# Clustered attention with a gated feed-forward part: P as the stationary operand of P times V, a column of ones beside V, and a turn by DMA

## The chip, the cores and the metric

The kernel runs on one core of a Trainium2 chip. The core has a matrix engine (TensorE: PE in the profile, with its weight loads listed apart as PEld), a vector engine (DVE), a scalar engine (ACT), a general engine (GpSimd: POOL), a synchronisation engine that issues transfers (SP), and 16 DMA engines. Work lies in SBUF (128 partitions); matmuls write into PSUM. The metric is device time in microseconds (us) of one execution, and the time of a kernel is the median of its runs.

## The reference

Four batches of eight heads, 768 tokens, head size 64. Queries and keys are assigned to the nearest of 16 centroids of their head; a query sees only keys of its own cluster. What follows is a feed-forward part over the heads side by side.

```python
q_assign = np.argmax(np.einsum('bhsd,hcd->bhsc', q_n, c_n), axis=-1)
k_assign = np.argmax(np.einsum('bhsd,hcd->bhsc', k_n, c_n), axis=-1)
mask = q_assign[:, :, :, None] == k_assign[:, :, None, :]
scores = np.where(mask, scale * (q @ k^T), -1e9)
attn = softmax(scores)                     # over keys
x = (attn @ v).transpose(0, 2, 1, 3).reshape(3072, 512)
h = x @ w_in                               # 512 -> 2048
return (h / (1 + exp(-h))) @ w_out         # 2048 -> 512
```

## The kernel before

**Tiles.** A pair p is two heads of one batch (16 pairs, four to a batch). A unit n is one pair and one third of its queries (256 of 768 tokens): 48 units, in the order of the list `units`; batch 0 has an order of its own (`SEQ0`). A chunk c is one batch and one third of its tokens (256 tokens, all 512 columns): 12 chunks, each the sum of four units.

**Steps of a unit.** Q and K come as nat, are split into a high and a low half (hl, lines 96 to 103) and turned into abt (features on partitions; by PE for pairs 0 to 3, by DMA at L113 for the others). The logits against the centroids (psL, L156) lead through a chain on DVE (lt, mx, oht, ohu) to one-hot rows beneath abt, so that a single matmul gives scores and mask. Then three steps of `qk` (L214) give st, keys on partitions and queries along the free axis, and `exp` on ACT (L220) turns each st into a P of 128 keys x (2 key tiles x 2 heads x 256 queries) in half precision.

**P times V** (`pv`, L222 to 253) works on two units at once, m. The stationary operand is a 128x32 piece of V (vt, L231) and P streams past, 256 columns each time, into one of four groups of 32 columns of the array: 48 matmuls for the pair of units. The output pv has features on partitions and tokens along the free axis, as the feed-forward part wants it. The softmax sums zz come from a stationary tile of ones of 128x32: 24 matmuls (L248), or, where m is in FAST (1, 2 and 23), 48 (L240), which give each sum on all the partitions where it is needed. Then:

- plain pairs: DVE copies pv to osb (L257) and takes the reciprocal rz of zz (L261); SP writes four rows of it to DRAM as rzd (L265) and reads them back spread over partitions as rzb (L276); POOL (in some places DVE) multiplies osb by rzb into xt (L289).
- FAST pairs: DVE takes the reciprocal over all partitions (rzb, L281) and multiplies straight from pv (L289).

**Feed-forward.** With all four units of a chunk in xt, `unit_a` (L305) makes ph with w_in as the stationary operand, ACT tanh (L311), DVE the gate gt (L314), `unit_b` (L327) makes po with gt as stationary operand and w_out streaming, DVE halves it into ot (L336) and SP stores it (L340). Chunks 10 and 11 (LATE) have their po in buffers of st.

**The order** is made by a list scheduler at build time (`Piece`, `run`, L401 to 502). Each step is a piece with the engines that may take it, a planned length, the pieces it comes after, the buffers it takes and gives, and a rank; at each planned moment an engine takes the ready piece of lowest rank. On the chip each engine works off its list in that order, and a piece that is not ready holds up what stands behind it on the same engine. PE fills planned gaps ahead of the first ph with `keep_warm` matmuls (warm, L297). The planned lengths set only the order.

Transfers: SP issues q, k, the turns by DMA, the one-hot rows, rzd, rzb and the stores; POOL issues v (L88, converting to half precision), w_in (L680) and w_out (L685). Pools of buffers that matter here: moe (PSUM, 3; shared by pv, zz, ph, the turns on PE and some logits), st (PSUM, 2), P (12), xt (5).

Of the kernel before, what the change touches and what calls it, by code (L numbers as in the profile page):

```python
# [11 lines left out]
f32 = mybir.dt.float32  # L12
f16 = mybir.dt.float16
# [6 lines left out]
def kernel(  # L20
# [47 lines left out]
    vts = [const.tile([128, 2, NJ, D], f16, name=f"vt{n}") for n in range(NV)]  # L68
    ones = const.tile([128, 32], f16, name="ones")
# [7 lines left out]
    sts, Ps, pvs, zzs, osbs, rzs, rzbs, xts, gts, phs, tns, pos, ots = ({} for _ in range(13))  # L77
# [8 lines left out]
    def load_v(p):  # L86
        b, r = divmod(p, HB)
        nc.gpsimd.dma_start(  # L88
            vts[p % NV].rearrange("p h j d -> p h (j d)"), v[b, 2 * r : 2 * r + 2].rearrange("h (p j) d -> p h (j d)", j=NJ)
        )  # L90
# [131 lines left out]
    def pv(m, fast):  # L222
        pvt = pvs[m] = ps.tile([128, 2, UQ], f32, name="pv", tag="moe", bufs=3)
        zz = zzs[m] = ps.tile([128, 2, UQ], f32, name="zz", tag="moe", bufs=3)
        kts = [(s, a) for s in range(3) for a in range(2)]
        quarters = [(h, e) for h in range(2) for e in range(2)]
        for j in range(2):
            p = units[2 * m + j][0]
            for s, a in kts:
                for h, e in quarters:  # L230
                    nc.tensor.matmul(  # L231
                        pvt[D * h + 32 * e : D * h + 32 * e + 32, j, :], vts[p % NV][:, h, 2 * s + a, 32 * e : 32 * e + 32],
                        Ps[2 * m + j, s][:, a, h, :], start=(j == 0 and (s, a) == kts[0]), stop=((s, a) == kts[-1]),
                        skip_group_check=True,
                    )
        if fast:
            for j in range(2):
                for s, a in kts:
                    for h, e in quarters:
                        nc.tensor.matmul(  # L240
                            zz[D * h + 32 * e : D * h + 32 * e + 32, j, :], ones, Ps[2 * m + j, s][:, a, h, :],
                            start=(j == 0 and (s, a) == kts[0]), stop=((s, a) == kts[-1]), skip_group_check=True,
                        )
        else:
            for s, a in kts:
                for h, j in quarters:
                    g = D * h + 32 * j
                    nc.tensor.matmul(  # L248
                        zz[g : g + 32, 0, :], ones, Ps[2 * m + j, s][:, a, h, :], start=((s, a) == kts[0]), stop=((s, a) == kts[-1])
                    )  # L250
        for j in range(2):
            for s in range(3):
                Ps.pop((2 * m + j, s))

    def pv_out(m):
        osb = osbs[m] = mp.tile([128, 2, UQ], f32, name="osb", bufs=4)
        nc.vector.tensor_copy(osb, pvs.pop(m))  # L257

    def z_recip(m):
        rz = rzs[m] = mp.tile([128, UQ], f32, name="rz", bufs=2)  # L260
        nc.vector.reciprocal(rz, zzs.pop(m)[:, 0, :])  # L261

    def z_in(m):
        rzd = dr.tile([4, UQ], f32, name="rzd", bufs=4)
        nc.sync.dma_start(rzd, rzs[m][0:128:32])  # L265
        rzs[m] = rzd

    def rzb_of(m):
        if m not in rzbs:
            rzbs[m] = mp.tile([128, 2, UQ], f32, name="rzb", bufs=3)  # L270
        return rzbs[m]

    def z_bcast(m):
        rzb, rzd = rzb_of(m), rzs.pop(m)
        for h in range(2):
            nc.sync.dma_start(  # L276
                rzb[D * h : D * h + D].rearrange("p j x -> p (j x)"), rzd[2 * h : 2 * h + 2].rearrange("(o j) x -> o (j x)", o=1).to_broadcast([D, 2 * UQ])
            )

    def z_fast(m, j):  # L280
        nc.vector.reciprocal(rzb_of(m)[:, j], zzs[m][:, j])  # L281

    def z_mul(m, j, eng, fast):
        p, u = units[2 * m + j]
        b, r = divmod(p, HB)
        c = b * U + u
        if c not in xts:
            xts[c] = mp.tile([128, NR, UQ], f16, name="xt", bufs=5)
        eng.tensor_tensor(  # L289
            out=xts[c][:, r, :], in0=(pvs if fast else osbs)[m][:, j, :], in1=rzbs[m][:, j, :], op=ALU.mult  # L290
        )
# [7 lines left out]
    def unit_a(c, f):  # L299
        if f == 0:  # L300
            gts[c] = mp.tile([128, NFB, UQ], f16, name="gt", bufs=2)
        ph = phs[c, f] = ps.tile([128, 2, UQ], f32, name="ph", tag="moe", bufs=3)
        for e in range(2):
            for r in range(NR):
                nc.tensor.matmul(  # L305
                    ph[:, e, :], win_s[:, r, ts(2 * f + e, 128)], xts[c][:, r, :], start=(r == 0), stop=(r == NR - 1)
                )
# [79 lines left out]
    def centroid_out(eng):  # L387
        copy = eng.copy if eng is nc.scalar else eng.tensor_copy
        for i, dst in enumerate((wh, wl)):
# [5 lines left out]
            "st": 2, "P": 12, "osb": 4, "rz": 2, "rzd": 4, "rzb": 3, "xt": 5, "gt": 2, "tn": 3, "ot": 2}  # L395
# [113 lines left out]
    LEAD, LEAD_V, LEAD_IN = 28, 22, 36  # L509
    FR0 = (-400, -285, -290, -280)  # L510
    RPV = -3
# [3 lines left out]
    FAST = (1,2,23)  # L515
# [23 lines left out]
    nc.vector.memset(ones, 1.0)  # L539
# [80 lines left out]
    exps, pvl, muls = {}, {}, {}  # L620
# [6 lines left out]
    def value_loads(p):  # L627
        b = p // HB
        casts[p] = [Piece(
            {"POOL": 0.74}, lambda e: load_v(p), ([last_pv[p - NV]] if p >= NV else []) + ([nat_in[HB - 1, 1]] if b == 0 else []), (), rank=-7.3 + p if b == 0 else p,  # L630
            when=from_slot(begins[p] - LEAD_V) if b else None, dma=(0.393, 2.2),
        )]

    for n, (p, u) in enumerate(units):
# [10 lines left out]
        if n % 2 == 0:  # L645
            continue
        m, fast = n // 2, n // 2 in FAST
        two = units[n - 1 : n + 1]
        tiles = [("moe", ("pv", m)), ("moe", ("zz", m))]
        x = Piece(  # L650
            {"PE": 2.82 if fast else 2.18}, lambda e, m=m, fast=fast: pv(m, fast),
            [exps[i] for i in range(3 * n - 3, 3 * n + 3)] + [y for o, _ in two for y in casts[o]], tiles,
            [("P", i) for i in range(3 * n - 3, 3 * n + 3)], rank=-20,
        )
        for o, _ in two:
            last_pv[o] = x
        early = n < 12
        if fast:
            zs = [
                Piece({"DVE": 1.72}, lambda e, m=m, j=j: z_fast(m, j), [x], [("rzb", m)], tiles[1:], rank=-350) for j in range(2)  # L660
            ]
            on, give, rank = {"DVE": 0.35}, tiles[:1] + [("rzb", m)], -300
        else:
            o = Piece({"DVE": 0.69}, lambda e, m=m: pv_out(m), [x], [("osb", m)], tiles[:1], rank=RPV if early else -3)
            x = Piece({"DVE": 1.72}, lambda e, m=m: z_recip(m), [x], [("rz", m)], tiles[1:], rank=RPV if early else -3)
            x = Piece({"SP": 0.5}, lambda e, m=m: z_in(m), [x], [("rzd", m)], [("rz", m)], rank=-4, dma=(0.01, 2.5))
# [77 lines left out]
```

## Time and profile before

| what | value |
|---|---|
| median of 3 runs | 340.08 us (339.46 to 340.91) |
| the profiled execution | 341.08 us, of which the span from first to last instruction is 339.1 |
| granted TensorE clock, mean | 0.995 |
| stores of the output after the last matmul (335.5 to 339.1) | 3.6 us |
| DVE: reciprocals of zz, L261 and L281 | 36.7 and 10.1 us busy |
| POOL: multiplies into xt, L289 | 31.6 us busy |
| DMA: packets | 62080, 43.05 MB |

A row of the profile names engine, line, operation, what it writes and reads, the shape and a count; a group's row has busy time, mean length in ns, and the idle time of the engine ahead of it with what ended that. Rows of the timeline begin with start and length in us. PE lists matmuls with their whole latency, so the rate is read from starts, not from lengths.

### The profile page before, as it was taken

Reading aid. Unit: us, or ns where it says so; the run is one execution under the profiler, and the core shown is the slowest. Engines: PE = TensorE matmul, PEld = TensorE weight load, DVE = VectorE, ACT = ScalarE, POOL = GpSimd, SP = SyncE. Lnnn points to the kernel's source line nnn. Section 1 sums busy time; section 2 is a strip of 40 time slices with the busy share of each in tenths; the row PEclk is TensorE's granted clock in tenths of the full one; section 3 lists DMA queues with packets and bytes.
Section 4 is the critical chain, followed back from the end, with each engine's and each line's share of the span. In section 5 each row is a group of like instructions: output and inputs, shape, how many; then the busy total and the mean of one; then the engine's idle time right before and its main releaser. Section 6 shows DMA issues by size and latency. Waiting matters only on the chain.

```text
span 339.1 us, 9192 instructions
## 1 busy us (share of the span) xinstructions
PE 319.2 (94%) x3956; PEld 232.5 (69%) x3956; DVE 227.0 (67%) x318; ACT 237.0 (70%) x275; POOL 51.9 (15%) x74
## 2 busy tenths in 40 slices
PE   7677987999998999999999999999999999999994
PEld 4455775777765777777777767777677687686651
DVE  5999979789566696457568895547544365266631
ACT  5895776966686868658779678758777786873430
POOL 4730010021103210130120320131011001000000
PEclk9999999999997999999999999999999999999999
DMA  7999999637399911435679671473210110210101
GB/s 236 286 239 254 225 175 216 126 74 194 80 279 258 200 37 57 100 90 90 200 232 244 128 163 46 74 143 65 74 44 34 62 45 21 64 64 2 62 33 62
DMA packets 62080, 43.05 MB, mean 127 GB/s; under 512 B 40580, under 2 KB 55768, under 8 KB 62040
## 3 DMA queue, kind: packets, MB, share of 16 engines
q1 hardware_dynamic: 55000, 35.13, 39.7%
q0 software_dynamic: 7040, 7.34, 13.6%
q8 instruction: 31, 0.51, 0.6%
q14 instruction: 9, 0.07, 0.1%
HBM read 32.80 MB, written 6.38 MB: 116 GB/s over the span
## 4 chain that ended last, share of the span: by engine, by line
PE 78%; DVE 12%; DMA 7%; issue 1%; SPq 1%; POOL 0%; ACT 0%; DVEq 0%; POOLq 0%
PE ph L305 25%; PE po L327 23%; PE st L214 15%; PE pv L231 8%; PE zz L248 4%; DVE hl L103 3%; DMA rzb<-rzd 3%; PE psL L156 2%; DMA rzd<-rz 2%; DMA nat<-in_q_dram 2%; DVE abt L206 1%; DVE ohu L188 1%; DVE rzb L281 1%; DVE lt L163 1%; DVE ot L336 1%
## 5 line engine op out<-in xcount | busy, mean ns | idle before, releaser
L220 ACT ACTIVATE P<-st,bias 128x1024 f16<-128x1024 f32 x144 | 156.5, 1113 | 53.7 <-PE st L214 53.3
L314 DVE SCALAR_TENSOR_TENSOR gt<-tn,ph 128x512 f16<-128x512 f32 x96 | 64.8, 684 | 54.4 <-ACT tn L311 53.7
L305 PE MATMUL ph<-xt,win_s 128*128 128x256 f16 x768 | 97.6, 275 | 2.8 <-POOL xt L289 1.5
L327 PE MATMUL po<-wout_s,gt 128*128 128x512 f16 x384 | 95.7, 379 | 1.1 <-DVE ot L336 1.1
L214 PE MATMUL st<-abt 80*128 80x256 f16 x576 | 84.6, 273 | 5.5 <-ACT P L220 2.2
L305 PEld LDWEIGHTS <-win_s 128*128 128x128 f16 x768 | 75.6, 98 | 20.1 <-issue 3.3
L311 ACT ACTIVATE tn<-ph,zbias 128x512 f32<-128x512 f32 x96 | 65.2, 686 | 30.3 <-PE ph L305 25.8
L214 PEld LDWEIGHTS <-abt 80*128 80x128 f16 x576 | 53.7, 97 | 29.4 <-issue 11.5
L289 POOL TENSOR_TENSOR xt<-osb,rzb 128x256 f16<-128x256 f32 x39 | 31.6, 829 | 238.0 <-DMA rzb<-rzd 219.5
L327 PEld LDWEIGHTS <-gt 128*128 128x128 f16 x384 | 37.3, 97 | 30.8 <-issue 1.8
L261 DVE RECIPROCAL rz<-zz 128x256 f32<-128x256 f32 x21 | 36.7, 1749 | 0.0
L231 PE MATMUL pv<-P,vt 128*32 128x256 f16 x1152 | 35.9, 273 | 0.0
L103 DVE SCALAR_TENSOR_TENSOR hl<-nat,hl 128x768 f16<-128x768 f32 x32 | 31.7, 1021 | 4.4 <-ACT hl L96 4.2
L231 PEld LDWEIGHTS <-vt 128*32 128x32 f16 x1152 | 28.6, 97 | 5.4 <-issue 4.6
L336 DVE TENSOR_SCALAR ot<-po 128x512 f32<-128x512 f32 x24 | 16.5, 686 | 22.6 <-PE po L327 22.5
L257 DVE COPY osb<-pv 128x512 f32<-128x512 f32 x21 | 14.5, 690 | 12.7 <-PE pv L231 12.5
L248 PE MATMUL zz<-P,ones 128*32 128x256 f16 x504 | 17.4, 273 | 0.0
L297 PE MATMUL warm<-idle,ident 128*128 128x256 f16 x74 | 13.3, 309 | 1.4 <-POOL ident masks.py:199 1.4
L248 PEld LDWEIGHTS <-ones 128*32 128x32 f16 x504 | 13.5, 97 | 0.3
L96 ACT ACTIVATE hl<-nat 128x768 f16<-128x768 f32 x14 | 11.7, 840 | 1.8 <-DMA nat<-in_q_dram 1.6
L88 POOL DMA_DIRECT2D vt<-in_v_dram x16 | 12.0, 748 | 5.9 <-PE pv L231 3.3
L281 DVE RECIPROCAL rzb<-zz 128x256 f32<-128x256 f32 x6 | 10.1, 1722 | 1.4 <-PE zz L240 1.4
(56 smaller groups left out, 139.7 us busy)
## 6 DMA issues: line engine op xcount, KB each, us to landing
nat<-in_q_dram SPq DMA_DIRECT2D x16, 384.0 KB
nat<-in_k_dram SPq DMA_DIRECT2D x16, 384.0 KB, 4.8
out_dram<-ot SPq DMA_DIRECT2D x24, 256.0 KB, 2.7
rzb<-rzd SPq DMA_DIRECT2D x42, 128.0 KB, 4.1
vt<-in_v_dram POOLq DMA_DIRECT2D x16, 192.0 KB, 4.9
win_s<-in_moe_w_in_dram POOLq DMA_DIRECT2D x4, 512.0 KB, 14.4
wout_s<-in_moe_w_out_dram POOLq DMA_DIRECT2D x4, 512.0 KB, 23.3
abt<-oh SPq DMA_DIRECT2D x48, 24.0 KB, 1.8
```

The lines of the kernel that those rows point to most:

```text
L103: nc.vector.scalar_tensor_tensor(out=hl[:, :, 1, :], in0=nat, scalar=128.0, in1=hl[:, :, 0, :], op0=ALU.mult, op1=ALU.subtract)
L214: nc.tensor.matmul(st[:, a, h, :], ab[0:K, 1, h, ts(2 * s + a, 128)], ab[0:K, 0, h, ts(u, UQ)], start=True, stop=True)
L220: nc.scalar.activation(out=P, in_=sts.pop((n, s)), func=AF.Exp, bias=bias32, scale=ESC)
L231: nc.tensor.matmul(pvt[D * h + 32 * e : D * h + 32 * e + 32, j, :], vts[p % NV][:, h, 2 * s + a, 32 * e : 32 * e + 32], Ps[2 * m + j, s][: ...
L248: nc.tensor.matmul(zz[g : g + 32, 0, :], ones, Ps[2 * m + j, s][:, a, h, :], start=((s, a) == kts[0]), stop=((s, a) == kts[-1]))
L261: nc.vector.reciprocal(rz, zzs.pop(m)[:, 0, :])
L289: eng.tensor_tensor(out=xts[c][:, r, :], in0=(pvs if fast else osbs)[m][:, j, :], in1=rzbs[m][:, j, :], op=ALU.mult)
L305: nc.tensor.matmul(ph[:, e, :], win_s[:, r, ts(2 * f + e, 128)], xts[c][:, r, :], start=(r == 0), stop=(r == NR - 1))
L311: nc.scalar.activation(out=tn, in_=phs[c, f], func=AF.Tanh, bias=zbias, scale=0.5)
L314: nc.vector.scalar_tensor_tensor(out=gts[c][:, 2 * f : 2 * f + 2, :], in0=tns.pop((c, f)), scalar=1.0, in1=phs.pop((c, f)), op0=ALU.add, o ...
L327: nc.tensor.matmul(pos[c, s], gts[c][:, fc, ts(s, 128)], wout_s[:, fc, :], start=(fc == 0), stop=(fc == NFB - 1))
L336: eng.tensor_scalar(out=ot, in0=pos.pop((c, s)), scalar1=0.5, scalar2=None, op0=ALU.mult)
```

## The change

P becomes the stationary operand. For each unit (not each pair of units) 24 matmuls each load a 128x128 tile of P (128 keys x 128 queries) and stream 65 columns past it: the 64 columns of V of that head and key tile, and a column of ones. The output pv has tokens on partitions, and its column 64 is the softmax sum of that token. So zz, its matmuls, the way through DRAM and the multiplies on POOL are gone. On DVE `normalise` takes the reciprocal of four columns (2 token tiles x 2 heads) and multiplies pv by it into xh (tokens on partitions, half precision). xh must be turned into xt, features on partitions: `x_dma` does this on SP with one DMA transpose for a whole chunk, or, for chunks 0 and 11 (XPE), `x_pe` with two times four transposes on PE and `x_out` with two copies on DVE or ACT. V lies in rows of 72 elements of which 64 are loaded and one is set to ones by POOL at the start; a pair's V is now loaded by two DMAs of 128 x 6 rows of 64 elements. The buffers osb, rz, rzd and rzb go; xh (3) comes; xt has 4 instead of 5. The loads of V start 16 st steps ahead of their use rather than 22 (LEAD_V).

```diff
-    vts = [const.tile([128, 2, NJ, D], f16, name=f"vt{n}") for n in range(NV)]
-    ones = const.tile([128, 32], f16, name="ones")
+    VW = 72
+    vts = [const.tile([128, 2, NJ, VW], f16, name=f"vt{n}") for n in range(NV)]
...
-        nc.gpsimd.dma_start(
-            vts[p % NV].rearrange("p h j d -> p h (j d)"), v[b, 2 * r : 2 * r + 2].rearrange("h (p j) d -> p h (j d)", j=NJ)
-        )
+        for h in range(2):
+            nc.gpsimd.dma_start(vts[p % NV][:, h, :, 0:D], v[b, 2 * r + h].rearrange("(p j) d -> p j d", j=NJ))
...
-    def pv(m, fast):
...
+    def pv(n):
+        p, u = units[n]
+        out = pvs[n] = ps.tile([128, 2, 2, D + 1], f32, name="pv", tag="moe", bufs=3)
+        for s in range(3):
+            P = Ps.pop((n, s))
+            for a in range(2):
+                for h in range(2):
+                    for e in range(2):
                         nc.tensor.matmul(
+                            out[:, e, h, :], P[:, a, h, ts(e, 128)], vts[p % NV][:, h, 2 * s + a, 0 : D + 1],
+                            start=(s + a + h + e == 0), stop=(s == 2 and a == 1), skip_group_check=True,
                         )
+    def normalise(n):
...
+        nc.vector.reciprocal(rz, out[:, :, :, D])
+        nc.vector.tensor_tensor(
+            out=xhs[c][:, :, r], in0=out[:, :, :, 0:D], in1=rz.unsqueeze(3).to_broadcast([128, 2, 2, D]), op=ALU.mult
+        )
+    def x_dma(c):
+        nc.sync.dma_start_transpose(xt_of(c).rearrange("p e r x -> p (e r) x"), xhs.pop(c).rearrange("p e r h d -> p (e r h d)"))
+    def x_pe(c, e):
+        xp = xps[c, e] = ps.tile([128, NR, 128], f16, name="xp", tag="moe", bufs=3)
+        for r in range(NR):
+            nc.tensor.transpose(xp[:, r, :], xhs[c][:, e, r].rearrange("p h d -> p (h d)"), ident)
+    def x_out(c, e, eng):
+        copy = eng.copy if eng is nc.scalar else eng.tensor_copy
+        copy(xt_of(c)[:, e], xps.pop((c, e)))
...
-    LEAD, LEAD_V, LEAD_IN = 28, 22, 36
+    LEAD, LEAD_V, LEAD_IN = 28, 16, 36
...
-    FAST = (1,2,23)
+    XPE = (0, 11)
...
+    for vt in vts:
+        nc.gpsimd.memset(vt[:, :, :, D : D + 1], 1.0)
```

With the pieces the scheduler's order changes. The next two pieces are from DVE's list before, and after, from the copies of the one-hot rows of batch 0's last pair (abt from ohu) towards the first xt; hl, from nat, is the split of batch 1's Q and K.

```order
L206 TENSOR_SCALAR abt_380<-ohu_615 16x768 x4
L257 COPY osb_641<-pv_504 128x512
L261 RECIPROCAL rz_652<-zz_505 128x256
L98 TENSOR_SCALAR hl_667<-nat0_473 128x12x64
L98 TENSOR_SCALAR hl_680<-nat1_477 128x12x64
L98 TENSOR_SCALAR hl_781<-nat0_499 128x12x64
L98 TENSOR_SCALAR hl_786<-nat1_502 128x12x64
L98 TENSOR_SCALAR hl_789<-nat0_580 128x12x64
L103 SCALAR_TENSOR_TENSOR hl_667<-nat0_473,hl_667 128x12x64
L281 RECIPROCAL rzb_800<-zz_684 128x256 x2
L289 TENSOR_TENSOR xt_835<-pv_683,rzb_800 128x256 x2
L289 TENSOR_TENSOR xt_848<-osb_641,rzb_792 128x256
```

```order
L205 TENSOR_SCALAR abt_385<-ohu_614 16x768 x4
L97 TENSOR_SCALAR hl_639<-nat0_541 128x12x64
L97 TENSOR_SCALAR hl_666<-nat1_562 128x12x64
L242 RECIPROCAL rz_675<-pv_641 128x4
L243 TENSOR_TENSOR xh_487<-pv_641,rz_675 128x2x128
L102 SCALAR_TENSOR_TENSOR hl_639<-nat0_541,hl_639 128x12x64
L102 SCALAR_TENSOR_TENSOR hl_666<-nat1_562,hl_666 128x12x64
L97 TENSOR_SCALAR hl_727<-nat0_569 128x12x64
L97 TENSOR_SCALAR hl_729<-nat1_572 128x12x64
L242 RECIPROCAL rz_740<-pv_702 128x4
L243 TENSOR_TENSOR xh_487<-pv_702,rz_740 128x2x128
```

The reciprocals of 256 columns and the multiplies into xt are replaced by short pairs of a reciprocal of 4 columns and a multiply into xh, one pair of instructions for each unit, spread between the splits. Two more such pairs (units 0 and 1) stand earlier, inside the routing of the last two pairs of heads. On PE the first ph stands behind 20 groups of st (of four matmuls each) in place of 25.

On SP's list, from the last loads of batch 1 on, before and after:

```order
L83 DMA nat_580<-in_q_dram 128x2x384
L83 DMA nat_582<-in_k_dram 128x2x384
L265 DMA rzd<-rz 4x256
L276 DMA rzb<-rzd 64x512 x2
L83 DMA nat_807<-in_q_dram 128x2x384
L113 DMA_TRANSPOSE abt<-hl 128x12x128
L83 DMA nat_959<-in_k_dram 128x2x384
L113 DMA_TRANSPOSE abt<-hl 128x12x128 x5
```

```order
L83 DMA nat_579<-in_q_dram 128x2x384
L83 DMA nat_586<-in_k_dram 128x2x384
L83 DMA nat_690<-in_q_dram 128x2x384
L112 DMA_TRANSPOSE abt<-hl 128x12x128
L83 DMA nat_738<-in_k_dram 128x2x384
L112 DMA_TRANSPOSE abt<-hl 128x12x128 x6
L253 DMA_TRANSPOSE xt<-xh 128x8x128
L112 DMA_TRANSPOSE abt<-hl 128x12x128
```

The way of the sums through DRAM is gone from SP, and the turn of chunk 1 stands among the turns of batch 1's Q and K. POOL's list before and after, from the end of the centroids' split:

```order
L88 DMA vt_75<-in_v_dram 128x2x384
L88 DMA vt_76<-in_v_dram 128x2x384
L88 DMA vt_77<-in_v_dram 128x2x384
L88 DMA vt_78<-in_v_dram 128x2x384
L680 DMA win_s<-in_moe_w_in_dram 128x2048 x4
L685 DMA wout_s<-in_moe_w_out_dram 128x4x512 x2
L88 DMA vt_79<-in_v_dram 128x2x384
L685 DMA wout_s<-in_moe_w_out_dram 128x4x512 x2
L88 DMA vt_80<-in_v_dram 128x2x384
```

```order
L89 DMA vt_75<-in_v_dram 128x6x64 x2
L89 DMA vt_76<-in_v_dram 128x6x64 x2
L89 DMA vt_77<-in_v_dram 128x6x64 x2
L89 DMA vt_78<-in_v_dram 128x6x64 x2
L642 DMA win_s<-in_moe_w_in_dram 128x2048 x4
L647 DMA wout_s<-in_moe_w_out_dram 128x4x512 x4
L89 DMA vt_79<-in_v_dram 128x6x64 x2
L89 DMA vt_80<-in_v_dram 128x6x64 x2
```

Eight issues for V stand where four stood, all of w_in and w_out behind them, and the V of batch 1's first two pairs behind all of w_out.

127 lines of the change are left out of this document (33 added, 94 removed).

## The prediction

> **What bounds the kernel now.** I read the page first (busy shares, slices, the chain that ended last), then busy time by stretches, then the timeline of TensorE.
>
> ```profile
> span 339.1 us, 9192 instructions
> PE 319.2 (94%) x3956; PEld 232.5 (69%) x3956; DVE 227.0 (67%) x318; ACT 237.0 (70%) x275; POOL 51.9 (15%) x74
> PE ph L305 25%; PE po L327 23%; PE st L214 15%; PE pv L231 8%; PE zz L248 4%; DVE hl L103 3%; DMA rzb<-rzd 3%; PE psL L156 2%; DMA rzd<-rz 2%; DMA nat<-in_q_dram 2%; DVE abt L206 1%; DVE ohu L188 1%; DVE rzb L281 1%; DVE lt L163 1%; DVE ot L336 1%
> ...
> 0.00:54.30 54.30, 42.01 (x600) 31.36 (x601) 47.12 (x85) 41.84 (x50) 13.99 (x26) 1.00 1.06 235
> 250.00:304.80 54.80, 54.80 (x668) 41.34 (x657) 28.21 (x35) 41.13 (x49) 5.22 (x7) 1.00 0.14 49
> 304.80:335.50 30.70, 29.44 (x263) 18.44 (x260) 15.04 (x22) 9.12 (x13) 0.73 (x1) 1.00 0.09 35
> ```
>
> The last three rows are stretches: the bounds, then length, busy us of PE, PEld, DVE, ACT, POOL, then granted clock, DMA share and GB/s. There are two stages. Up to 54.3 us PE is no limit (42.0 of 54.3, warm-up matmuls included), while DVE is busy for 47.1. From 54.3, where the first matmul of the feed-forward part (ph) starts, to the last matmul at 335.5, PE hardly rests: the end is the start of that stage plus the PE work that is then left plus the holes. So the change is to be priced by what it does to PE work after the first ph, to the time of the first ph, and to the holes.
>
> **PE work of P times V.** Timeline rows: start, length, engine, line, what, count.
>
> ```profile
> 155.42 1.04 PE L305 MATMUL ph<-xt,win_s 128*128 128x256 f16 x8
> ...
> 156.73 1.03 PE L327 MATMUL po<-wout_s,gt 128*128 128x512 f16 x4
> 157.59 1.04 PE L305 MATMUL ph<-xt,win_s 128*128 128x256 f16 x8
> ...
> 160.64 0.60 PE L214 MATMUL st<-abt 80*128 80x256 f16 x4
> 161.18 1.49 PE L231 MATMUL pv<-P,vt 128*32 128x256 f16 x48
> 162.50 0.83 PE L248 MATMUL zz<-P,ones 128*32 128x256 f16 x24
> 163.25 0.61 PE L214 MATMUL st<-abt 80*128 80x256 f16 x4
> ...
> 306.74 1.50 PE L231 MATMUL pv<-P,vt 128*32 128x256 f16 x48
> ...
> 309.47 1.04 PE L327 MATMUL po<-wout_s,gt 128*128 128x512 f16 x4
> ...
> 15.27 0.49 PE L118 MATMUL ptt<-ident,hl 128*128 128x128 f16 x6 [0.80 <-ACT abt L123]
> ...
> L118 PE MATMUL ptt<-ident,hl 128*128 128x128 f16 x96 | 6.9, 219 | 3.3 <-ACT abt L123 1.9 <-DVE abt L123 0.9 <-DVE hl L103 0.4
> ```
>
> The lengths hold the pipeline's latency, so starts count. A pair of units costs PE 163.25 - 161.18 = 2.07 us, and another 0.1 where the array changes from full width to 32-column tiles (the four st before it are worth 0.44 and end by that at 161.08): **2.17 per pair**, and 309.47 - 306.74 + 0.1 = **2.83** for a pair with 48 matmuls of zz instead of 24 (three pairs, FAST). Twenty plain pairs and one of those stand behind the first ph: 20 x 2.17 + 2.83 = **46.2 us**.
>
> After, a unit is 24 matmuls, each with its own load of a 128x128 tile of P, and streams only 65 columns. No row shows 65 columns. From the rows: six matmuls of 128 columns take 0.49 us, of which the last one alone is 0.22, so they start (0.49 - 0.22) / 5 = 54 ns apart, 55 with the rounding; eight ph and the four st behind them, all of 256 columns, take 156.73 - 155.42 = 1.31 us, 109 ns each; four po of 512 take 157.59 - 156.73 = 0.86, 215 ns each. That is about 0.42 ns per column and 2 ns more, which gives 65 columns **29 ns**, if the load of P keeps up. For the load:
>
> ```profile
> 309.47 0.11 PEld L327 LDWEIGHTS <-gt 128*128 128x128 f16 x2 [0.21 <-issue]
> ...
> L305 PEld LDWEIGHTS <-win_s 128*128 128x128 f16 x768 | 75.6, 98 | 20.1 <-issue 3.3
> L231 PEld LDWEIGHTS <-vt 128*32 128x32 f16 x1152 | 28.6, 97 | 5.4 <-issue 4.6
> ```
>
> Two loads of 128x128 that wait for nothing between them fit into 0.11 us though each lasts 97, so the second starts about 15 ns behind the first; and a load of 128 columns lasts no longer than one of 32 (98 against 97 ns). The bounds are therefore 29 ns from below and 55 ns, the closest that a load and a matmul of full width are seen to follow each other, from above. I take 29, because the upper row is set by its own 128 columns and the 15 ns of the load fit under 29. Then 42 units x 24 x 29 ns = **29.2 us**, without the change of array shape: 17.0 saved behind the first ph. The turn of chunk 11 on PE (8 transposes of 55 ns) gives back **0.4**.
>
> Here the Trainium skill speaks against the change. "TensorE: Matmul & The Clock Gate", section "Back-to-back issue gap", says that in a stream of load and matmul pairs 128 columns sustain about 81 ns each, 25 above the lone matmul, because the load takes its share. By that a 65-column pair would be some 54 ns (an estimate), and the saving would be gone. The 55 ns that this trace shows at 128 columns speak against the rule.
>
> **When the first ph starts.** Rows of PE, ACT and DVE.
>
> ```profile
> 39.20 1.49 PE L231 MATMUL pv<-P,vt 128*32 128x256 f16 x48
> 40.52 1.48 PE L240 MATMUL zz<-P,ones 128*32 128x256 f16 x48
> 46.76 0.60 PE L214 MATMUL st<-abt 80*128 80x256 f16 x4 [0.19 <-ACT P L220]
> 54.34 0.49 PE L305 MATMUL ph<-xt,win_s 128*128 128x256 f16 x3
> ...
> 32.28 8.35 ACT L220 ACTIVATE P<-st,bias 128x1024 f16<-128x1024 f32 x8 [0.80 <-PE st L214]
> 42.58 6.13 ACT L220 ACTIVATE P<-st,bias 128x1024 f16<-128x1024 f32 x6 [1.95 <-PE st L214]
> ...
> 36.62 0.69 DVE L257 COPY osb<-pv 128x512 f32<-128x512 f32 x1
> 37.23 1.75 DVE L261 RECIPROCAL rz<-zz 128x256 f32<-128x256 f32 x1
> 42.23 3.36 DVE L281 RECIPROCAL rzb<-zz 128x256 f32<-128x256 f32 x2
> ...
> L353 DVE RECIPROCAL cr<-cy 128x1 f32<-128x1 f32 x2 | 0.3, 163 | 0.4 <-ACT cy L363 0.4
> L289 DVE TENSOR_TENSOR xt<-pv,rzb 128x256 f16<-128x256 f32 x6 | 2.1, 384 | 0.0
> ```
>
> Before, the first ph stands behind 25 groups of st; after, behind 20. The 20th starts now at 46.8, paced by ACT at 1.04 us (8.35 / 8), with a gap of 1.95 on ACT that the 2.7 us block of pv and zz at 39.2 causes. Blocks of 24 x 29 ns = 0.7 us hide under one step of ACT, so that gap goes. Against it, two normalisations now stand ahead of the routing of the last two pairs. One is a reciprocal of 4 columns (163 ns at one column; (1749 - 163) / 255 = 6 ns for each further one: 0.18) and a multiply (0.38), so 0.57, and together with the reordering about 0.8 us. The 20th st comes at 46.8 - 1.95 + 0.8 = 45.7; behind it stand its own 0.44, one pv of 0.7, and the wait for normalisation, turn and copy of chunk 0, which I put at 1.2 (a normalisation and a copy of PSUM at 0.6 each): the first ph at **48.0**, 6.3 earlier. The reciprocals of zz on DVE (one more such pair stands between 52.4 and 55.8) are gone from that way. But five groups of st (5 x 0.44 = 2.2) move behind it: **4.1** gained. What is late next is win_s:
>
> ```profile
> q0 software_dynamic: 710, 0.52, 68.3%
> ...
> q1 hardware_dynamic: 144, 0.03, 9.8%
> ...
> L680 POOL DMA_DIRECT2D win_s<-in_moe_w_in_dram x4: 538/567/651, 10.9 to 12.6; - x4
> DMA to landing us min/median/max: 10.7/14.4/18.1
> ```
>
> Its last piece lands at about 12.6 + 18.1 = 30.7, behind four loads of V. A load of V turns from 256 packets (128 partitions x 2 heads) into 1536 (x 6 tiles) of 256 bytes at the source. The rows q0 and q1 are packets and their share of 16 engines in two windows. The 144 of q1 (0.7 to 2.2 us) are craw, rows of 256 bytes from HBM and a few ends: 9.8% of 16 x 1.5 us, so 16 ns each. The 710 of q0 (10 to 15 us), V's of today and some of win_s, take 68.3% of 16 x 5 us, 77 ns each. Four loads cost 4 x 256 x 77 / 16 = 4.9 us of all DMA engines now; after, between 4 x 1536 x 16 / 16 = 6.1 and, at 77, 29.6. I take the craw row, the one of that size: win_s at some 32, covered by the 16 us up to 48. POOL's issues double too (8 for 4); it loses its multiplies for that and has nothing else to do. Its six memsets of the ones column stand ahead of ident, at a time when it waits for the norm of the centroids anyway.
>
> **Holes.** The stage of 281.1 us holds 46.2 of pv and zz, 96 x 0.87 of ph, 96 x 0.87 of po, 119 x 0.44 of st and six logits blocks of 1.41, 274 in all; 7 are holes. Their largest:
>
> ```profile
> 56.12 0.71 PE L305 MATMUL ph<-xt,win_s 128*128 128x256 f16 x5 [1.29 <-DVE xt L289]
> 103.75 2.43 PE L305 MATMUL ph<-xt,win_s 128*128 128x256 f16 x13 [1.19 <-POOL xt L289]
> 147.95 1.41 PE psL L156 x32
> ...
> rzb<-rzd SPq DMA_DIRECT2D x42, 128.0 KB, 4.1
> abt<-hl SPq DMA_TRANSPOSE x24, 4.4
> ```
>
> The waits for xt behind the sums' way are worth 1.3 + 1.2, and 13 matmuls in 2.43 us instead of 12 x 0.11 + 0.27 = 1.6 another 0.8: 3.3 in all. Their path (reciprocal 1.75, a DMA out, 4.1 for the DMA back, a multiply on POOL) becomes 0.57 on DVE and one DMA turn, for which abt gives 4.4. It is shorter, but stands in SP's queue ahead of turns of K and Q, loads and stores, which then wait for the last unit of a chunk. I count half: **1.7**.
>
> **Sum.** The profiled execution took 341.08 (span 339.1 and 2.0 around it). 341.1 - 17.0 + 0.4 - 4.1 - 1.7 = 318.7. The median of the runs (340.08) is 1.0 below that execution: **318** rounded, 6.5% faster. DVE (one reciprocal of 1.75 and a copy of 0.69 less for each pair, two times 0.57 more) and POOL gain besides, but nothing waits for them there, so I cost that at nothing.
>
> **Rivals.** *A, the load is not hidden:* the pair takes 55 ns like the full-width row. Then P times V costs 42 x 24 x 55 = 55.4, 9.2 more than now, and the time is 340.1 + 9.2 + 0.4 - 4.1 - 1.7 = **344**, slower. It decides from (46.2 - 0.4 + 4.1 + 1.7) / 1008 = 51 ns. For it: no row shows the two closer. Against it: the 15 ns between loads, and equal lengths at 32 and 128 columns. *B, V's short packets:* at 77 ns win_s lands at 30.7 + 24.7 = 55.4, the first ph waits 7.4 longer: **325**. For it: DMA is saturated up to 54 us (share 1.06). Against it: craw. *C, ACT becomes the limit in places:* from 250 to 304.8 ACT is busy 41.1 of 54.8 and would have the same work in about 51. A wait of 0.19, as ACT's P causes at 46.76, for each of 42 units is 8 us: **326**. That the change doesn't do what it says I rule out: its matmuls stand in the order as 24 to a unit.
>
> **How the numbers follow.** Forecast (312 to 324) 0.64; B 0.11; C 0.13; A 0.08; and 0.04 for a mixture that lands within 0.5%, about what a measurement of this kernel can tell from no change. The range runs from 312 (all holes gone, the first ph two more us earlier) to 331 (B or C, with 5 more for pairs of 34 ns); A stays outside. Faster 0.88, same 0.04, slower 0.08.
>
> **What would show it.** Starts of pv matmuls 29 ns apart and blocks of 0.7; the first ph near 48; win_s landed before 40; PE full from there on. Over 50 ns, or a first ph past 55 that waits for win_s or vt, and I am wrong.

## The result and the profile after

The changed kernel takes **322.0 us** (median of 4 runs, 319.5 to 323.8) against 339.8 for the kernel before in the same session: 0.9475 of the time, 95% interval 0.9395 to 0.9554. In the next session, as the control of the experiments, it took 321.2 (0.9436, 0.9396 to 0.9476). The forecast was 318, in a range of 312 to 331.

First the page of the changed kernel (span, busy shares, the chain that ended last, two groups), then what the trace answers on the tile win_s.

```profile
span 322.0 us, 7812 instructions
...
PE 302.5 (94%) x3316; PEld 225.5 (70%) x3316; DVE 190.2 (59%) x356; ACT 239.3 (74%) x279; POOL 35.3 (11%) x57
...
PE ph L276 25%; PE po L298 24%; PE st L213 16%; PE pv L229 9%; DMA abt<-hl 6%; PE psL L155 3%; DMA nat<-in_q_dram 2%; DMA xt<-xh 2%; DVE hl L102 1%; DVE abt L205 1%; DVE ohu L187 1%; DVE lt L162 1%; DVE hl L97 1%; DVE mx L173 1%; DVE oht L180 1%
...
L229 PE MATMUL pv<-vt,P 128*128 128x65 f16 x1152 | 43.3, 193 | 0.2 <-ACT P L219 0.2
L229 PEld LDWEIGHTS <-P 128*128 128x128 f16 x1152 | 41.8, 98 | 2.1 <-ACT P L219 0.3
```

```profile
L642 POOL DMA_DIRECT2D win_s<-in_moe_w_in_dram x4: 528/534/552, 15.1 to 18.0; - x4
...
DMA to landing us min/median/max: 10.1/13.2/16.3
```

In the chain zz, rzd and rzb are gone, and a new entry has come: the turn of hl into abt by DMA, with 6%, which did not stand in the chain before. win_s has landed by 18.0 + 16.3 = 34.3, well ahead of the first ph.

The stretches (bounds, length, busy us of PE, PEld, DVE, ACT, POOL, granted clock, DMA share, GB/s):

```profile
0.00:47.68 47.68, 37.64 (x460) 28.24 (x461) 40.17 (x84) 38.88 (x48) 19.04 (x37) 0.96 1.24 236
47.68:53.30 5.62, 2.35 (x26) 1.86 (x22) 1.12 (x4) 3.84 (x5) 0.00 (x0) 1.00 1.61 170
53.30:57.00 3.70, 3.69 (x26) 2.77 (x27) 2.01 (x3) 1.10 (x2) 0.00 (x0) 0.54 1.35 107
...
60.00:155.00 95.00, 95.00 (x1101) 71.92 (x1099) 63.52 (x113) 74.91 (x88) 11.43 (x14) 1.00 0.81 138
155.00:166.00 11.00, 10.14 (x112) 7.58 (x111) 3.10 (x7) 7.97 (x10) 1.63 (x2) 1.00 1.08 234
...
225.00:280.00 55.00, 55.00 (x593) 41.52 (x592) 22.74 (x47) 42.48 (x48) 0.00 (x0) 1.00 0.16 43
```

From 60 to 300 us PE is full but for one wait (0.86 us at 163.4). The trouble lies between 47.7 and 57: PE is busy for 2.35 of 5.62 us, and then, full, runs at a clock of 0.54. The timeline of PE, a piece there and two further on:

```profile
46.95 0.89 PE L229 MATMUL pv<-vt,P 128*128 128x65 f16 x24
47.68 1.04 PE L276 MATMUL ph<-xt,win_s 128*128 128x256 f16 x8
48.55 0.60 PE L213 MATMUL st<-abt 80*128 80x256 f16 x4
48.99 1.04 PE L276 MATMUL ph<-xt,win_s 128*128 128x256 f16 x8
53.31 1.64 PE L276 MATMUL ph<-xt,win_s 128*128 128x256 f16 x8 [3.28 <-DVE xh L243]
...
150.17 0.90 PE L229 MATMUL pv<-vt,P 128*128 128x65 f16 x24
150.90 1.02 PE L298 MATMUL po<-wout_s,gt 128*128 128x512 f16 x4
...
164.25 1.05 PE L276 MATMUL ph<-xt,win_s 128*128 128x256 f16 x8 [0.86 <-DMA xt<-xh]
```

and that of DVE at the same place:

```profile
52.14 0.56 DVE L97 TENSOR_SCALAR hl<-nat 128x768 f16<-128x768 f32 x1 [5.25 <-DMA abt<-hl]
52.62 0.17 DVE L242 RECIPROCAL rz<-pv 128x4 f32<-128x4 f32 x1
52.83 0.42 DVE L243 TENSOR_TENSOR xh<-pv,rz 128x256 f16<-128x256 f32 x1
```

A unit of P times V takes 150.90 - 150.17 = 0.73 us from start to start, 30.4 ns per matmul. PE's wait of 3.28 us at 50.0 is named after xh: the next ph needs a buffer of moe, and the normalisation that writes xh is what gives back the one that pv held. But xh itself was late by the instruction ahead of it: a split of batch 1's Q or K (hl) that stood for 5.25 us until a buffer of hl came free, which a turn by DMA was still reading. The normalisation, 0.59 us of work, stood behind it in DVE's list.

**The account.** Before and after, from the two profiled executions:

| term | forecast | measured |
|---|---|---|
| first ph (54.34 before) | 48.0: -6.3 | 47.68: -6.7 |
| five groups of st behind it (119, then 124) | +2.2 | +2.2 |
| 42 units of P times V (46.2 before) | 29.2: -17.0 | 42 x 0.73 = 30.7: -15.5 |
| turn of chunk 11 on PE | +0.4 | +0.4 |
| holes from the first ph to the last matmul | 7 to 5.3: -1.7 | 7 to 9.2: **+2.2** |
| the end and what lies around the span | 0 | +0.1 |
| sum | -22.4 | -17.3 |

The last matmul ends at 318.0, so that stage has 318.0 - 47.7 = 270.3 us; its work is 30.7 + 192 x 0.87 + 124 x 0.44 + 6 x 1.41 + 0.4 = 261.1, which leaves 9.2. Of these, 3.28 and 0.86 are the two waits shown and 1.1 two waits near the end that the kernel before has too; the stretch at 0.54 costs 1.7 (3.70 x 0.46); the other 2.3 are not traced to a cause. The execution took 323.8, 17.3 less than 341.1.

### The profile page after: what moved, and what is told of

Its sections match the earlier page's. It is cut to its first block, busy times and chain, and to the rows that moved or that the text cites. A ratio compares the mean times of both kernels' runs of the same rounds, so it can differ in the third digit from the quotient of the medians.

```text
span 322.0 us, 7812 instructions
## 1 busy us (share of the span) xinstructions
PE 302.5 (94%) x3316; PEld 225.5 (70%) x3316; DVE 190.2 (59%) x356; ACT 239.3 (74%) x279; POOL 35.3 (11%) x57
## 4 chain that ended last, share of the span: by engine, by line
PE 78%; DMA 9%; DVE 9%; ACT 1%; issue 1%; SPq 1%; DVEq 0%
PE ph L276 25%; PE po L298 24%; PE st L213 16%; PE pv L229 9%; DMA abt<-hl 6%; PE psL L155 3%; DMA nat<-in_q_dram 2%; DMA xt<-xh 2%; DVE hl L102 1%; DVE abt L205 1%; DVE ohu L187 1%; DVE lt L162 1%; DVE hl L97 1%; DVE mx L173 1%; DVE oht L180 1%
## 5 line engine op out<-in xcount | busy, mean ns | idle before, releaser
L89 POOL DMA_DIRECT2D vt<-in_v_dram x32 | 26.5, 833 | 174.0 <-PE pv L229 165.2
L229 PE MATMUL pv<-vt,P 128*128 128x65 f16 x1152 | 43.3, 193 | 0.2 <-ACT P L219 0.2
L229 PEld LDWEIGHTS <-P 128*128 128x128 f16 x1152 | 41.8, 98 | 2.1 <-ACT P L219 0.3
L102 DVE SCALAR_TENSOR_TENSOR hl<-nat,hl 128x768 f16<-128x768 f32 x32 | 29.8, 956 | 2.8 <-ACT hl L95 2.5
L242 DVE RECIPROCAL rz<-pv 128x4 f32<-128x4 f32 x48 | 8.6, 178 | 28.0 <-PE pv L229 27.6
L243 DVE TENSOR_TENSOR xh<-pv,rz 128x256 f16<-128x256 f32 x48 | 20.4, 424 | 1.7
L97 DVE TENSOR_SCALAR hl<-nat 128x768 f16<-128x768 f32 x19 | 10.4, 556 | 5.3 <-DMA abt<-hl 5.2
L155 PE MATMUL psL<-abt,wh 128*32 128x512 f16 (+1 forms) x128 | 10.5, 340 | 0.7 <-DVE abt L122 0.4
L187 DVE STREAM_TRANSPOSE ohu<-oht 128x768 f16<-128x768 f16 x10 | 9.8, 977 | 0.9 <-DVE oht L180 0.5
L117 PE MATMUL ptt<-ident,hl 128*128 128x128 f16 x96 | 7.7, 235 | 2.7 <-ACT abt L122 1.9
```

Of the source, the lines that this page charges most:

```text
L89: nc.gpsimd.dma_start(vts[p % NV][:, h, :, 0:D], v[b, 2 * r + h].rearrange("(p j) d -> p j d", j=NJ))
L102: nc.vector.scalar_tensor_tensor(out=hl[:, :, 1, :], in0=nat, scalar=128.0, in1=hl[:, :, 0, :], op0=ALU.mult, op1=ALU.subtract)
L155: nc.tensor.matmul(psL[g : g + 32, 0 : hi - lo], w, x[:, lo:hi], start=first, stop=last)
L229: nc.tensor.matmul(out[:, e, h, :], P[:, a, h, ts(e, 128)], vts[p % NV][:, h, 2 * s + a, 0 : D + 1], start=(s + a + h + e == 0), stop=(s = ...
L243: nc.vector.tensor_tensor(out=xhs[c][:, :, r], in0=out[:, :, :, 0:D], in1=rz.unsqueeze(3).to_broadcast([128, 2, 2, D]), op=ALU.mult)
```

## Experiments

All but one (7) start from the changed kernel. Times are medians, and the ratios in brackets are to runs of the kernel before in the same session (340.6, 339.6 and 340.4 us in the three sessions; experiments 1, 2, 4 and 5 are from the first). Two questions are open: what sets the 30 ns of a 65-column matmul, and what made the holes. On the first, theory M says that the columns do, its rivals that the load does, or that PE had slack to hide the difference. On the second, theory R says that the ring of hl buffers joins the late turns to PE, theory P that V's short packets make the turns late, and theory H, which came up with the first four runs, that PE's standstills halve its clock in the early stage; the rivals are that the hole only moves, and that it is nothing to the time.

**1. Control.** The changed kernel as it is.

> The changed kernel once more, as the control beside the others on this chip. By its earlier runs about 322 us (319.5 to 323.8), with the hole of about 3.3 us on PE after the second block of ph (near 50 us), where DVE waits some 5 us for a turn of K or Q (abt from hl).

321.2 us (320.6 to 322.2). Its profile differs from the first one: the first ph is at 50.72 instead of 47.68, and there is no hole behind it (264.1 us from there to the last matmul, holes 3.0 instead of 9.2; span 318.8). One program, two courses: an early ph that runs into a hole, and a late one that doesn't. The wait of DVE for a turn is there too, shorter, but PE has work in that time:

```profile
51.65 0.56 DVE L97 TENSOR_SCALAR hl<-nat 128x768 f16<-128x768 f32 x1 [1.92 <-DMA abt<-hl]
```

So a profile without a hole near 50 doesn't by itself show that a repair worked. What delayed the ph is seen in experiment 6.

**2. 128 columns.** `vts[...][:, h, 2*s+a, 0 : D+1]` becomes 128 columns from the same place of a flattened tile, pv becomes 128 wide.

> Each matmul of P times V streams 128 columns instead of 65 (the rest is the neighbouring rows of the V tile, and is not used); the order of PE is unchanged. Theory M (columns set the spacing, the load of P is hidden, PE work passes to the end one for one): matmuls 55 to 56 ns apart for 29, so 42 x 24 x 26 ns = 26 us more, about 348. Rival L (a load and a matmul share the time, the page's 81 ns at 128 columns): 42 x 24 x 52 ns, about 374. Rival O (PE has slack, the added work is partly hidden): below 340.

346.2 us (1.0159, 1.0098 to 1.022). The timeline's piece:

```profile
159.16 1.50 PE L230 MATMUL pv<-vt,P 128*128 128x128 f16 x24
160.50 1.03 PE L299 MATMUL po<-wout_s,gt 128*128 128x512 f16 x4
```

160.50 - 159.16 = 1.34 us, 56 ns per matmul. 42 x (1.34 - 0.73) = 25.6 us more. The time went up by 25.0, and in the profiles the stage from the first ph to the last matmul by 25.7 (289.8 for the control's 264.1): what P times V costs behind the first ph passes to the end one for one, and there is no slack on PE.

**3. 33 columns.** Half of V's columns are left out, so this kernel is for its timing only.

```diff
-  vts[p % NV][:, h, 2 * s + a, 0 : D + 1],
+  vts[p % NV][:, h, 2 * s + a, 32 : D + 1],
```

> The changed kernel with 33 columns instead of 65 streaming past each P tile: half of the value columns (0 to 31) is left out and the other half is used twice, so the normalisation is two products of 128 columns instead of one of 256. Theory M (the columns alone set the spacing, 65 in 30.4 ns and 128 in 56): 33 columns in 15 to 17 ns, 0.36 to 0.41 us per unit, 13 to 15 us less PE work after the first ph, of which ACT (74% busy) lets through most: 307 to 312. Rival L (the load of a 128x128 tile sets a floor of nearly 29 ns, which 65 columns happened to touch): spacing 27 to 29 ns, time 319 to 322.

317.6 us in one run, with the hole near 50 (2.83) as in the profile after.

```profile
164.13 0.76 PE L229 MATMUL pv<-vt,P 128*128 128x33 f16 x24
164.74 1.02 PE L299 MATMUL po<-wout_s,gt 128*128 128x512 f16 x4
```

0.61 us per unit, 25 ns per matmul: neither expectation, and nearer to rival L's. With half of the columns gone only 5 ns went. So 128, 65 and 33 columns take 56, 30 and 25 ns: by columns at first, then hardly. That 25 is a floor, of which 65 columns stay just clear, is how I read it; there is no run below 33 columns.

**4. A sixth buffer of hl** (`name="hl", bufs=5` to 6, the order of all work unchanged).

> One more buffer for hl (6 for 5), the order of every engine unchanged. Theory R (the ring of five hl buffers is where a late turn stops DVE, and with it the normalisation that ph waits for through the PSUM buffers): the DVE wait of 5.2 us and the PE hole of 3.3 us near 50 us go, and with the hole the half clock after it: 3.3 plus some 1.8 of slower matmuls, so about 317. Rival S (DVE would wait for the late transfers at the next instruction anyway, or the PE hole has another cause): the hole stays or moves by a microsecond, 321 to 322.

320.7 us (0.9411, 0.9378 to 0.9445). The first ph is at 48.2, nearly as early as in the first profile, and there is no hole near 50 (no idle of PE over 0.3 us from 45 to 58); DVE's wait for a buffer comes at a later split and is shorter:

```profile
57.50 0.56 DVE L97 TENSOR_SCALAR hl<-nat 128x768 f16<-128x768 f32 x1 [1.61 <-DMA abt<-hl]
```

The turns themselves are as late as ever (12.6 us at worst, 12.2 in the first profile), so it is the buffer that joins them to PE. The median moved by 0.5 us only, within the intervals; the 317 that was expected did not come.

**5. V loads of pairs 4 and 5 held** until the last turn of pair 5 is down (a copy of one column on POOL ahead of them that reads it).

```diff
+        if p == HB:
+            nc.gpsimd.tensor_copy(mp.tile([32, 1], f16, name="after_turn"), abt_of(HB + 1)[0:32, 1, 2 * NJ - 1, 0:1])
```

> The V loads of batch 1's first two pairs (four DMAs of short rows) wait, by a small copy on POOL that reads it, for the last turn of batch 1's second pair; nothing else is moved. Theory P (the short V packets, landing at 40 to 53 us, are what makes the turns of 41 to 52 us late): the first turn lands in some 5 us instead of over 10, the hole near 50 us goes, about 317 to 318. Rival Q (the turns are late because they are issued 4 us earlier than in the kernel before and meet w_out and the q and k loads): the first turns stay late, the hole stays, 321 to 323.

320.1 us (0.9397, 0.9356 to 0.9438). The turns land in 6.8 us at worst instead of 12.2 (9.7 in the control), no split of DVE waits for one any more, and there is no hole near 50; the first ph stands at 49.9. The 1.1 us against the control are within the intervals, and the 317 to 318 of theory P did not come. The two queues between 46 and 52 us (packets, MB, share of 16 engines), after the change and in the combination (9, below) that also holds these loads:

```profile
q1 hardware_dynamic: 1662, 0.57, 93.8%
q0 software_dynamic: 1738, 0.24, 70.5%
```

```profile
q1 hardware_dynamic: 3363, 1.17, 126.9%
q0 software_dynamic: 13, 0.01, 1.1%
```

After the change 1738 short packets of V, only 0.24 MB, take 70.5% of 16 x 6 us, 39 ns each, while SP's queue with the turns (q1) moves 0.57 MB, half of what it moves without them. (The two shares add up to 164%: the times of packets overlap, so 100% is not a ceiling.) In the kernel before, q0 has 10 packets in these 6 us.

**6. Idle matmuls where PE stands still** (12 each ahead of the third block of ptt, the first st, and the first st of pair 2).

```diff
+        if (n, s) in ((0, 0), (2, 0)):
+            keep_warm(12)
...
```

> The changed kernel with 12 idle matmuls (1.3 us at full clock) put ahead of each of the three PE instructions that waited longest in the first 34 us of its profile (the third block of six ptt, the first st, the first st of pair 2), all three behind waits that are there anyway. Theory H (the half clock comes some 2 to 4 us after PE has stood still for over 1.3 us in one piece; without such pieces it isn't halved before the first ph; each halved stretch of 3.4 us makes the PE work that lies in it twice as long and the first ph later): granted clock 1.00 in all of 10 to 48, first ph 47.0 to 48.0, time 319 to 320.5, and a narrower spread over its runs than the control's 320.6 to 322.2. Rival N (PE's stillness has nothing to do with it; the clock is halved by the power of the DMAs or of the chip): half windows as in the control, time 321.0 to 322.0. Rival C (the filled waits were shorter than 1.3 us and the idle matmuls delay the first exp): first ph after 49, time 322 to 323.

322.7 us (0.949, 0.9459 to 0.9521): no gain; by the ratios 1.8 us worse than the control, within the intervals. But the clock did what theory H says. Stretches of PE alone (bounds, length, busy us, granted clock, DMA share, GB/s), the control first:

```profile
8.00:12.00 4.00, 2.10 (x20) 0.69 1.25 350
12.00:16.00 4.00, 4.00 (x42) 0.50 1.99 213
...
32.00:36.00 4.00, 2.04 (x15) 1.00 1.16 264
36.00:40.00 4.00, 3.74 (x27) 0.61 1.24 210
40.00:44.00 4.00, 4.00 (x37) 0.54 1.36 199
```

```profile
8.00:12.00 4.00, 3.65 (x47) 1.00 1.21 353
12.00:16.00 4.00, 3.30 (x49) 1.00 2.00 211
...
32.00:36.00 4.00, 3.01 (x23) 1.00 1.15 255
36.00:40.00 4.00, 3.71 (x50) 1.00 1.24 208
40.00:44.00 4.00, 3.79 (x69) 1.00 1.24 220
...
48.00:52.00 4.00, 1.50 (x15) 1.00 1.47 197
52.00:56.00 4.00, 4.00 (x44) 0.64 1.65 146
```

In the control two stretches in which PE works for 2.0 or 2.1 of 4 us run into some 7 us at half clock each; with the idle matmuls neither comes, and the first ph is at 46.7, 4.0 earlier than in the control (and 1.0 earlier than in the first profile, which has one such stretch, from 12.6 to 16.0). All of it is then lost: the earlier ph runs into the late turn (a hole of 2.5 at 49.1), and the half clock comes after that.

**7. V's short rows alone, in the kernel before** (rows of 72, two DMAs a pair).

> The kernel before with one part of the change alone: V is loaded into rows of 72, in two DMAs per pair with descriptors of 256 B instead of one with 3 KB (32 DMAs instead of 16, the products unchanged). Theory P (the short rows cost nothing by themselves in the middle of the program; they only hold up what shares the DMA engines in the first 15 us and around the last loads and turns before the first ph): first ph 54 to 56, time 340 to 343, ratio 1.00 to 1.008. Rival (the loads themselves are a cost of 7 us, rival B of the prediction): first ph after 58, time 347. Rival (no effect at all, the late turns of the changed kernel have another cause): turns of hl land within 5 us as in the kernel before, and the time is 340.0 to 340.5.

345.7 us, 1.018 (1.0136 to 1.0224): **6.1 us slower**. The size is that of the rival, the place that of theory P: the first ph is at 54.1, as before the change, and the loss comes behind it.

```profile
57.80 1.23 PE L304 MATMUL ph<-xt,win_s 128*128 128x256 f16 x5 [3.22 <-DVE xt L288]
```

This wait was 1.29 in the kernel before; half clock from 56 to 63 begins in it. On DVE the multiplies that it waits for are late because an earlier one, ahead of them on the list, waits 3.83 us for the sums' way through DRAM (rzb), against 1.88 before. In the two profiles the stage from the first ph on is 4.3 us longer (285.3 for 281.0), which the wait and the half clock cover; the medians differ by more. So a new form of V's loads that the sum had at nothing costs 6 us in the old surroundings.

**8. V loaded in one piece and spread by POOL** (a staging tile, then `nc.gpsimd.tensor_copy` into the rows of 72).

> The changed kernel with V loaded as before the change (one DMA per pair, 3 KB per partition in one piece) into a staging tile, and copied from there by POOL into the rows of 72 (about 1 us of POOL per pair, in which POOL issues no DMA); the planner puts a few blocks after the first ph in another order. Theory P (the short rows cost 6.1 us in the kernel before, through one late product ahead of the second ph block and a half-clock stretch behind it; in the changed kernel they cost the late turns of hl near 50 us in the same way): turns land within 6 us, no hole over 1 us between 45 and 60, time 317 to 319. Rival (holding back the V loads of pairs 4 and 5 alone has already taken what there was, 1.1 us of 321.2): 319.5 to 320.5. Rival (POOL's copies come late and hold up pv): a pv behind POOL in the waits, time over 321.

323.6 us (0.9518, 0.9472 to 0.9564), and the turns land in 10.6 at worst, with a hole of 2.83 at 52.2. That speaks against theory P as I had put it: the rows are long again, and the turns as late. Between 46 and 52 us:

```profile
q0 software_dynamic: 880, 0.65, 69.0%
q1 hardware_dynamic: 1281, 0.65, 55.7%
```

The software queue is as full there as with the short rows, now with 0.65 MB, because POOL's copies stand ahead of its issues: win_s is issued from 20.4 on instead of 15.1, and what follows moves with it. What the profiles with late turns have in common is therefore not the row but the **backlog of the software queue when batch 1's turns begin**; short rows are one way to it, late issues another. That is argued, not shown: experiment 5 shows that the turns come sooner when V's loads are held, but no run separates the form of the loads from their place. After the change the V of batch 1's first two pairs is issued from 25.4 to 35.4, behind all of w_out; before, at 17.5 and 24.9.

**9. The parts together.** Sixth buffer, held V loads, idle matmuls:

> The combination without the later rank of the first 12 normalisations: the sixth hl buffer, the V loads of pairs 4 and 5 held, and the idle matmuls (12, 12, 12); the order of all other work is that of the changed kernel. If the earlier exp chain (normalisations off batch 0's routing) carries the combination's 317.4: first ph near 47, time 319 to 320. If the turns in time and the full clock carry it (theories R, P and H): first ph at 46.5 to 47.5, no hole, no half clock, time 317.5 to 318.5. Alone, the idle matmuls gave a first ph at 46.7 and then a hole of 2.5 at 49.1 with half clock behind it, 322.7.

**317.6 us** (0.9332, 0.9298 to 0.9365). First ph at 46.0, no hole over 0.7 us but the one ahead of the last po that the kernel before has too, clock 1.00 in every stretch, the turns within 9.1, and no split of DVE waits for one:

```profile
0.00:46.00 46.00, 40.36 (x496) 30.85 (x497) 40.43 (x85) 38.69 (x48) 15.69 (x33) 1.00 1.20 241
46.00:60.00 14.00, 14.00 (x179) 11.49 (x179) 9.00 (x18) 13.83 (x17) 3.57 (x6) 1.00 1.32 196
```

The same, with the first 12 normalisations ranked behind batch 0's routing on DVE (`rank=-300` to -270) and 6 idle matmuls instead of 12 ahead of pair 2:

> Everything that the runs so far point to, together: the sixth hl buffer, the V loads of pairs 4 and 5 held until the turns of pair 5 are down, the idle matmuls of the run before (6 instead of 12 ahead of pair 2), and the first 12 normalisations ranked behind batch 0's routing on DVE, so that nothing stands between the rows abt L205 of a pair. Theory H with R and P: first ph at 46 to 47.5, no hole over 0.5 us after it but the tail's, granted clock 1.00 from 10 on, time 315.5 to 318. Rival (the first ph is bounded by ACT's exp chain, whose start is all that the normalisations moved, and a hole that goes comes back at the next late turn): 319 to 320.5, as each part alone.

317.4 us (0.9346, 0.9321 to 0.9372), first ph at 45.4: no difference that these runs can tell. The last one with the staged loads of 8 in place of the held ones:

> The combination with the staged V loads in place of the held ones: sixth hl buffer, idle matmuls, later normalisations, V loaded in one piece per pair and spread by POOL. Theory P: the same turns in time, and no held loads: first ph at 45 to 46.5, time 315.5 to 317.5. Rival (POOL's copies delay its other issues, win_s and w_out among them): win_s lands after 36 and the time is 318 to 320.

320.9 us (0.941, 0.9364 to 0.9456), 0.9 above the range of its rival, with win_s down by 36.2, as that said. In its profile the clock is half from 20.7 to 27.5, with the idle matmuls in place. So the combination without the rank is the version that beats both kernels, by 3.6 us against the control (by the ratios, 0.9436 and 0.9332, 3.5), clear of the intervals: more than its three parts alone (0.5, 1.1 and -1.5, none clear of noise) add up to. The profiles fit this: an earlier first ph was lost where a split then waited for a turn (experiment 6) and kept where none did (here). No run leaves one of the three parts out, so which of them the 3.6 needs is not shown.

**10. All chunks turned by PE** (`XPE = tuple(range(12))`), the DMA turn of the change undone.

> The changed kernel with all 12 chunks turned by PE (8 transposes of 128x128 each and two copies by DVE or ACT) instead of two by PE and ten by DMA. By the prediction's price for a turn on PE (0.4 us per chunk beside the copies) ten more cost 4 to 4.5 us, against which stand the waits for a turned chunk (0.86 at 164) and the DMA time that the turns take from those of hl: theory S (PE's work passes to the end): 324 to 326. Rival T (the late turns of hl come from the turns of x on the same queue): hole at 50 gone and time 320 to 322.

324.5 us in 2 runs (0.953, 0.9471 to 0.9589), 3.3 above the control, as theory S; the hole near 51 is still there (1.28) and the turns of hl land in 12.3 at worst, so the turns of x aren't what makes those of hl late.

## Why the prediction held, and where it did not

**P times V: right in mechanism, 1.5 us too low.** The saving is what the change is worth, and it passes to the end one for one (experiment 2). The sum had 29 ns; the starts are 29 apart in the median, but with some at 35 the mean is 30.4. That 29 was made of 0.42 ns per column and 2 more, with the load hidden; the run at 33 columns shows that such a line does not go on below (16 ns by it, 25 measured). The forecast lay 5 ns above those 25, of which its rows knew nothing: that the line still held at 65 was luck.

**Rival A, the load not hidden, is rejected**: 30 ns at 65 columns with a load of 128x128 each, and 56 only at 128 columns. The Trainium skill, "TensorE: Matmul & The Clock Gate", section "Back-to-back issue gap", gives 81 ns for pairs of a load and a 128-column matmul in a stream; in place of the 25.6 us that 128 columns cost here at 56 ns, 81 would have cost some 51 (an estimate by that page). The trace disagrees with that figure. The same section states a floor of about 25 ns for the issue of up to 64 columns; the 25 ns at 33 columns agree. Whether it is the issue or the load of P that makes it, no run here separates.

**The first ph: right** (47.7 for 48.0), by a reading that left out the clock. In the profiles of experiments 1, 4 and 5 and the first one it lies between 47.7 and 50.7, and the half-clock stretches ahead of it differ (one in the first, two in the control, each twice as long); the kernel before had none there. That the profiled run came within 0.3 of the forecast is in part luck. win_s was down by 34.3 (32 forecast).

**The holes: the step that failed.** "I count half: 1.7" was a gain; it became a loss of 2.2 in the profiled run. The way of the sums did get short, as said: 0.59 us on DVE for 0.57. But the prediction named only what stands behind the turn of x on SP, and not what stands *ahead* of the normalisation on DVE: the splits of batch 1, each of which needs one of five buffers of hl, and with that a turn by DMA that shares the engines with V. Two costs followed: the wait itself (3.28) and the half clock behind it, in which 3.7 us did the work of about 2. The control paid elsewhere: its holes are 3.0, a gain of 4.0, but its first ph is 2.7 later than forecast.

One of the waits that the prediction counted was also none for xt. The 13 matmuls in 2.43 us at 103.75 ran at half clock in the kernel before (0.83 is the mean of these 10 us, 0.57 that of 104 to 108), after the standstill of 1.19:

```profile
100.00:110.00 10.00, 8.51 (x54) 5.92 (x52) 6.83 (x9) 7.38 (x9) 3.33 (x3) 0.83 1.10 246
```

**Rival B, V's short packets: wrong way, nearly the right size.** The sum took 16 ns per packet from the row of craw; they took 39 in the window above (the bound was 77); craw had been read with the DMA engines at 9.8%, and that window has both queues at 164% together. win_s was covered, as forecast; the turns were not. In the kernel before, the same rows cost 6.1, against the 7.4 of the rival. In the changed kernel the price cannot be read alone, since the loads in long rows came at another time.

**Rival C, ACT:** ahead of pv, PE waits for P of ACT for 0.2 us in all (its group above). ACT is busy 42.48 of 55.0 late in the program, and is no limit.

The 317.6 of the combination looks like the forecast of 318, but only because its terms offset each other: 265.4 us behind the first ph, 261.1 of them work (1.5 more than forecast) and 4.3 holes (1.0 less), and a first ph at 46.0 (2.0 earlier, helped by the idle matmuls). The mechanism of the saving was right; what was missing was the cover for the splits ahead of the normalisation.

## What to carry to other kernels

When a step becomes short, look at what stands ahead of it in its engine's list: it now waits there, for buffers and transfers that had not mattered. Price a transfer's new form in engine time (packets by the ns of one, in the window where it runs) and follow the whole queue to the point where the next urgent transfer starts, not only to the next load. Try repairs together before dropping them: three that moved the time by 0.5, 1.1 and -1.5 us alone brought 3.6 together.

## What was not expected of the hardware

- **Standstills of one to three us were often followed by half clock, in a full program too.** After the change, 3.28 us of idle PE at 50.0 are followed by 53.3 to 57.0 at 0.54; in the run of the idle matmuls 2.5 at 49.1 by 52 to 56 at 0.64. Of shorter ones only some are followed by it: 1.36 us at 32.4 in the control was, 1.36 at 31.6 in the profile after was not. So the length of one standstill doesn't decide, and short ones can add up: in the profile of the combination with staged loads half clock begins at 20.7 behind waits of 0.79 us at most. In the two combinations of 317.4 and 317.6, with no standstill of 1.0 us behind the first matmul, the clock is 1.00 up to the last. In the 14 profiles, a half-clock stretch ahead of the last matmul lasts 3.4 or 6.8 us. "TensorE: Matmul & The Clock Gate", section "Part 1: The HAM clock gate (the "warmup" mystery)" of the Trainium skill, has half clock after an idle window of some 3.4 us; the 3.4 agree with the length of the slow stretches, but here less than half a window of idleness was enough at times (1.19 us at 102.6 in the kernel before).
- **A matmul with its own load of a 128x128 tile starts every 25 ns at 33 columns, 30 at 65, 56 at 128.** A full new stationary tile for each 65 columns costs hardly more than the columns (30.4 ns, where the line of the prediction's rows gives 29).
- **Little data can load the DMA engines heavily:** 0.24 MB in 1738 packets took 70.5% of 16 engines' time for 6 us, as the profile counts it, beside 93.8% of the other queue.
